# Folding phi's weights in two halves of TensorE's rows, two heads in each

## The chip, the cores and the metric

The kernel runs on one core of one Trainium2 chip. The metric is the device time of one execution in microseconds (us). Before the change three runs took 357.98 us in the median (357.31 to 358.96). The profiled execution is one more, with a time of its own.

## The reference, cut to what matters

Two branches, A and B, each compute linear attention with a learned feature map over the same x (2048 tokens, 448 features, 16 heads of 28), and a gate mixes them:

```python
qkv = (x @ wqkv)                                  # per branch; q, k, v of 16 heads x 28
pq = einsum("bhsd,hdf->bhsf", q, w_phi)           # per head 28 x 28
pk = einsum("bhsd,hdf->bhsf", k, w_phi)
phi_q = concat([softmax(pq), softmax(-pq)])       # and phi_k of pk
kv = einsum("bhsf,bhsd->bhfd", phi_k, v); z = phi_k.sum over s
o = einsum(phi_q, kv) / (einsum(phi_q, z) + 1e-6)
out = g * (oA @ woA) + (1 - g) * (oB @ woB),  g = sigmoid((x * gate_w).sum(-1))
```

w_phi acts on q and k head by head, so x @ wq followed by w_phi is one product with a folded weight: for each head, wq's 28 columns times w_phi's 28 x 28. The kernel computes these folded weights once, for k and for q of each branch (four folds), and then projects x with them.

## The kernel before, in words

**Order of the work.** One program, each engine runs its instructions in the order in which the kernel issues them (`tc.manual_schedule()`). The first loop runs over eight units of 256 tokens for branch A's k and v (state kv), a second loop over eight units does A's q, B's k and v and A's numerators, and a list of steps written by hand does B's queries and the output. Projections (`proj`, L181) are 22 matmuls of 448 or 450 columns per unit in fp32r. `kv_acc` (L245) makes 32 matmuls of 56 columns, whose results go to four strips of 32 PSUM partitions. `num` (L327) makes 32 matmuls of a 32 x 32 weight with 256 columns, in four strips of rows by four strips of columns.

**A fold.** `fold` (L159) takes a weight that lies transposed in SBUF: `wt`, 112 partitions (4 heads x 28) by 4 groups by 512 columns (448 input features and 64 repeated). Group g holds heads 4g to 4g+3. `bd` is a block-diagonal 112 x 112 matrix for each branch and group, made of w_phi by four multiplications with a mask (L399). For each pair of input chunks (c, c+1) and each group, `fold_mm` issues one fp32 matmul: weights are 112 rows x 128 columns of `wt`, the moving operand is `bd`, 112 columns, the result 128 x 112 of a PSUM bank, one bank for each chunk. `fold_out` copies the 128 x 896 result to an fp32r tile on ScalarE (L156) and writes the rest to a second one on VectorE (L157). The profile shows each fp32 matmul as two pairs of a weight load and a matmul, so a fold is 16 matmuls in the program and 32 pairs in the trace.

**The four folds and their sources.** Fold 1 (A's k) stands after the first v projection; its weights come by `load_wt` (L114, DMA L117) in two DMAs of 448 KB, behind the first loads of x and wv and ahead of x for tokens 256 to 511 (`load_x(0, 2, 4)`, xrb) on SP's queue. Fold 2 (A's q) stands in unit 1, fold 3 (B's k) in unit 3, fold 4 (B's q) in unit 0 of the second loop; each of their weights is one DMA of 896 KB, issued long before. The last one (into tile `ctr`) is issued in unit 5, between loads of `wos` and the store of a q tile (`qd`, L281).

**Queues.** SP and ScalarE issue the DMAs, each in its own order. The program gives the DMAs of both queues eight semaphores in turn, so a DMA is not issued before the one eight places ahead of it has landed. ScalarE issues the loads of wp (w_phi, L376) and mask (L377) before its first work, the table load and the split of x (L108).

Of the kernel before, what the change touches and what calls it, by code (L numbers as in the profile page):

```python
# [8 lines left out]
F32 = mybir.dt.float32  # L9
F32R = mybir.dt.float32r  # L10
AF = mybir.ActivationFunctionType
OP = mybir.AluOpType
AX = mybir.AxisListType

P = 128
S, D, H, DH = 2048, 448, 16, 28
# [3 lines left out]
HA = 2 * H  # L20
NP = H // 2
PF = 4 * DH
DG = D + 2
HP = 32
WARM = 21
# [24 lines left out]
def hedgehog_mix(ctx: ExitStack, tc: tile.TileContext, xd, wv, wkt, wqt, wphi, wo, cmask, cpmask, out):  # L50


    nc = tc.nc
# [24 lines left out]
    wp_ = ctx.enter_context(tc.tile_pool(name="wts", bufs=1))  # L78

    res = ctx.enter_context(tc.tile_pool(name="res", bufs=1, side="right"))  # L80
    wtb = [res.tile([P, 2048], F32, name=f"wtb{i}") for i in range(2)]
# [4 lines left out]
    start = ExitStack()  # L86
    raw = start.enter_context(tc.tile_pool(name="raw", bufs=1, side="right"))
    ident = raw.tile([P, P], F32, name="ident")
    make_identity(nc, ident)
    mask = raw.tile([PF, 4], F32, name="mask")  # L90
    wp = raw.tile([PF, 2, 4, HP], F32, name="wp")
    bd = wp_.tile([PF, 2, 4, PF], F32, name="bd")
    wk = [wp_.tile([P, 2, 4, D], F32R, name="wka"), wp_.tile([P, 2, 4, D], F32R, name="wkb")]
    wvs = [wp_.tile([P, 2, 4, DG], F32R, name="wva"), wp_.tile([P, 2, 4, D], F32R, name="wvb")]
    wq = [wp_.tile([P, 2, 4, D], F32R, name="wqa"), None]
# [6 lines left out]
    def load_x(g, lo, hi, eng=nc.sync):  # L102
        eng.dma_start(xraw[g][:, :, lo * P:hi * P], xd[:, g * GT + lo * P:g * GT + hi * P].rearrange("(c p) t -> p c t", p=P))

    def split_x(g, lo, hi, *parts):
        r, t, h = [a[:, :, lo * P:hi * P] for a in (xraw[g], xg[g], xg[g].bitcast(F32))]
        if 0 in parts:
            nc.scalar.activation(t[:, 0:4], r, AF.Copy)  # L108
        if 1 in parts:
            nc.gpsimd.tensor_tensor(t[64:P, 3], r[64:P, 3], h[64:P, 3], OP.subtract)  # L110
        if 2 in parts:
            nc.gpsimd.tensor_tensor(t[:, 4:7], r[:, 0:3], h[:, 0:3], OP.subtract)  # L112

    def load_wt(dst, src, n=4):  # L114
        wt = dst[:PF].rearrange("p (g c) -> p g c", g=4)
        for g in range(0, 4, n):
            nc.sync.dma_start(wt[:, g:g + n], src[g * PF:(g + n) * PF].rearrange("(g p) c -> p g c", p=PF))  # L117
        return wt

    def load_wv(b, c, n=2, eng=nc.sync):  # L120
        w = (DG, D)[b]
        if c % 2 == 0:
            t = raw.tile([P, 2, w], F32, name=f"wvr{c}")
            for i in range(2):
                wvr[c + i] = t[:, i]
            if n == 2:
                return eng.dma_start(t, wv[c * P:(c + 2) * P, b * DG:b * DG + w].rearrange("(c p) n -> p c n", p=P))
        eng.dma_start(wvr[c], wv[c * P:(c + 1) * P, b * DG:b * DG + w])

# [14 lines left out]
    def two_tile(i=None):  # L144
        if i is None:
            i = turn[0] = (turn[0] + 1) % 3
        return twos[i].tile([P, 2, 512], F32, name=f"two{i}")

    def fold_mm(b, wt, ps, g, c):
        for i in range(2):  # L150
            nc.tensor.matmul(ps[:, i, g * PF:(g + 1) * PF], wt[:, g, (c + i) * P:(c + i + 1) * P], bd[:, b, g],  # L151
                             start=True, stop=True)

    def fold_out(ps, dst, c):
        dh, dl = dst[:, 0, c:c + 2], dst[:, 1, c:c + 2]
        nc.scalar.activation(dh, ps[:, :, :D], AF.Copy)  # L156
        nc.vector.tensor_tensor(dl, ps[:, :, :D], dh.bitcast(F32), OP.subtract)  # L157

    def fold(b, wt, dst):  # L159
        for c in range(0, 4, 2):  # L160
            ps = two_tile()
            for g in range(4):
                fold_mm(b, wt, ps, g, c)
            fold_out(ps, dst, c)

    TERMS = [(c, 0, c) for c in range(3)] + [(4 + c, 0, c) for c in range(3)] + [(3, 0, 3)] + [(c, 1, c) for c in range(4)]
# [5 lines left out]
    def proj(u, w, ps, order=None):  # L172
        n = w.shape[3]
        for i, j in order or [(i, j) for i in range(2) for j in range(11)]:
            if i is None:
                warm(j)
                continue
            t = 2 * u + i
            x, o = xg[t // 4], (t % 4) * P
            xc, k, wc = TERMS[j]  # L180
            nc.tensor.matmul(ps[:, i, :n], x[:, xc, o:o + P], w[:, k, wc], start=j == 0, stop=j == 10)  # L181
        return ps
# [190 lines left out]
    load_x(0, 0, 1)  # L373
    load_wv(0, 0, 1, nc.scalar)
    load_wv(0, 1, 1)
    nc.scalar.dma_start(wp, wphi)  # L376
    nc.scalar.dma_start(mask, cmask)  # L377
    load_wv(0, 2, 1)
    load_wv(0, 3, 1)
    load_x(0, 1, 2)  # L380
    wt = load_wt(wtb[0], wkt[0], 2)
    load_x(0, 2, 4)
    load_x(1, 0, 4)
    for v in vs:
# [10 lines left out]
        high_wv(0, c)  # L395
        low_wv(0, c, nc.vector)
    split_x(0, 1, 2, 0, 1, 2)
    for q in range(4):
        nc.vector.tensor_scalar(bd[:, :, :, q * DH:(q + 1) * DH], wp[:, :, :, :DH], mask[:, q:q + 1], None, op0=OP.mult)  # L399
    pv = proj(0, wvs[0], two_tile(), TERMS0)  # L400
    split_x(0, 2, 4, 0, 1, 2)
    v_out(0, pv)
    fold(0, wt, wk[0])
    split_x(1, 0, 4, 0, 1, 2)
    v_out(1, proj(1, wvs[0], two_tile()))
# [25 lines left out]
    for u in range(NU):  # L431
# [29 lines left out]
        if u == 0:  # L461
            wtqa = load_wt(wtb[0], wqt[0])
            load_x(2, 0, 4)
            for c in range(0, 4, 2):
                load_wv(1, c)
        if u == 1:
            wtkb = load_wt(wtb[1], wkt[1])
            nc.sync.dma_start(wos.rearrange("g (a f) n -> g a (f n)", f=DH),
                              wo.rearrange("(a g f) n -> g a (f n)", g=4, f=DH))
# [21 lines left out]
        if u == 1:  # L491
            fold(0, wtqa, wq[0])
        if u == 3:
            fold(1, wtkb, wk[1])
# [11 lines left out]
    wq[1] = wp_.tile([P, 2, 4, D], F32R, name="wka")  # L506
    ca = wp_.tile([P, 2, 4, DG], F32, name="wva").rearrange("p x c n -> p (x c n)")
    ctr = [ca[:, :2048], None]
# [23 lines left out]
    for u in range(NU):  # L532
        k = NU + u
        f, m, n = u + 2, u + 1, u - 1
# [257 lines left out]
    for step in STEPS.split():  # L792
        name, _, arg = step.partition(".")
# [44 lines left out]
```

## Time and profile before

| | |
|---|---|
| median of three runs | 357.98 us |
| the profiled execution: time / span of its instructions | 359.09 us / 357.2 us |
| TensorE clock granted, mean | 0.998 |
| busy share PE / weight loads (PEld) / VectorE (DVE) / ScalarE (ACT) / GpSimd (POOL) | 97 / 85 / 76 / 34 / 73% |
| moved by DMA | 45.75 MB, 128 GB/s in the mean |
| matmuls of the four folds (L151) | 128 in the trace, 11.3 + 3.8 us busy |

The span runs from the first to the last instruction; the execution's time is 1.9 us longer. In the rows below, PEld is the weight load of TensorE and PE the matmul; `[0.77 <-POOL xg L112]` means that the engine was idle for 0.77 us and that POOL's instruction of line 112, which wrote xg, ended that. Rows ending in q (SPq, ACTq) are the issue of a DMA. "x32" is the number of merged instructions.

### The profile page before, as it was taken

To read this page: it belongs to the slowest core of one execution; us is meant where nothing else is said; L and a number is where in the kernel's file an instruction comes from. 1 tells how busy PE (TensorE), PEld (TensorE's weight loads), DVE (VectorE), ACT (ScalarE), POOL (GpSimd) and SP (SyncE) were. 2 spreads that over 40 slices of the span, in tenths; PEclk is the share of its full clock that TensorE was granted. 3 is DMA by queue.
4 is the path that set the end of the run, shared out by engine and by line. 5 is a ranking of instruction groups with operands and counts; after the bars stand their busy time and mean duration, and the time that the engine had idled before them with its cause. 6 is when DMAs were issued, how large, how long until landed. Compare 5 with 4: busy or idle time off the path is not lost.

```text
span 357.2 us, 8435 instructions
## 1 busy us (share of the span) xinstructions
PE 346.2 (97%) x3599; PEld 304.6 (85%) x3599; DVE 270.1 (76%) x312; ACT 121.8 (34%) x171; POOL 261.5 (73%) x226
## 2 busy tenths in 40 slices
PE   7999899999999999999999999999999999999995
PEld 6889789988987889798898989888888978888894
DVE  4118765643967749998989898899899999988840
ACT  4433532534054241315133131412224454434331
POOL 2453897497476606988889788886779999999850
PEclk9999999999999999999999999999999999999999
DMA  7795225300753402241313332249662461664111
GB/s 236 221 319 173 114 79 193 135 25 14 210 157 141 129 1 61 75 126 61 103 54 104 106 104 65 94 162 352 160 226 84 140 196 57 180 180 128 53 52 51
DMA packets 33733, 45.75 MB, mean 128 GB/s; under 512 B 11408, under 2 KB 27008, under 8 KB 33408
## 3 DMA queue, kind: packets, MB, share of 16 engines
q1 hardware_dynamic: 28688, 41.20, 36.9%
q10 hardware_dynamic: 5008, 4.02, 3.5%
q8 instruction: 28, 0.46, 0.5%
q14 instruction: 9, 0.07, 0.1%
HBM read 27.29 MB, written 19.53 MB: 131 GB/s over the span
## 4 chain that ended last, share of the span: by engine, by line
PE 65%; DMA 12%; POOL 8%; DVE 8%; issue 3%; ACT 2%; SPq 1%; ACTq 0%; POOLq 0%; DVEq 0%
PE two L181 39%; PE out L773 16%; PE two L327 4%; DMA qd<-uq 4%; POOL e L220 3%; PE kv L245 3%; DMA xrb<-in_xt 2%; POOL xg L112 1%; DMA wtb<-wos 1%; DVE sm L211 1%; DVE wtb L315 1%; ACT e L202 1%; DMA wp<-in_wphi 1%; DMA wod<-wtb 1%; PE two L151 1%
## 5 line engine op out<-in xcount | busy, mean ns | idle before, releaser
L181 PE MATMUL two<-wka,xg 128*128 128x448 f32 x352 | 73.8, 365 | 0.0
L181 PEld LDWEIGHTS two<-wka,xg 128*128 128x128 f32 x352 | 65.2, 188 | 5.6 <-issue 0.8
L220 POOL TENSOR_TENSOR e<-e,rs 128x896 f32<-128x896 f32 x32 | 53.9, 1706 | 19.1 <-DVE rs L212 19.1
L228 ACT ACTIVATE vs<-two 128x896 f32<-128x896 f32 x16 | 14.7, 920 | 97.6 <-PE two L181 97.6
L181 PE MATMUL two<-wva,xg 128*128 128x450 f32 x176 | 39.4, 373 | 1.9 <-ACT wva L131 1.0
L211 DVE TENSOR_REDUCE sm<-e 128x32 f32<-128x896 f32 x32 | 33.1, 1077 | 8.6 <-ACT e L202 8.6
L181 PE MATMUL two<-wqa,xg 128*128 128x448 f32 x176 | 38.0, 371 | 1.0 <-DVE wqa L157 1.0
L315 DVE STREAM_TRANSPOSE wtb<-xrb 128x2048 f32<-128x2048 f32 x16 | 36.6, 2290 | 2.3 <-ACT glog L230 2.3
L181 PEld LDWEIGHTS two<-wva,xg 128*128 128x128 f32 x176 | 32.8, 189 | 6.2 <-POOL xg L112 1.1
L181 PE MATMUL two<-wvb,xg 128*128 128x448 f32 x176 | 37.2, 366 | 0.0
L181 PE MATMUL two<-wkb,xg 128*128 128x448 f32 x176 | 36.5, 362 | 0.0
L181 PEld LDWEIGHTS two<-wqa,xg 128*128 128x128 f32 x176 | 32.4, 188 | 4.8 <-DVE wqa L157 1.4
L198 POOL TENSOR_TENSOR e<-mx,e 128x896 f32<-128x896 f32 x16 | 27.3, 1704 | 12.5 <-DVE mx L197 9.2
L181 PEld LDWEIGHTS two<-wvb,xg 128*128 128x128 f32 x176 | 33.0, 188 | 2.7
L181 PEld LDWEIGHTS two<-wkb,xg 128*128 128x128 f32 x176 | 33.0, 188 | 2.3
L773 PE MATMUL out<-wkb,e 128*128 128x448 f32 x154 | 34.7, 369 | 0.1
L202 ACT ACTIVATE e<-e 128x896 f32<-128x896 f32 x32 | 28.7, 945 | 17.7 <-POOL e L198 17.6
L773 PEld LDWEIGHTS out<-wkb,e 128*128 128x128 f32 x154 | 28.5, 188 | 4.1 <-issue 0.8
L305 POOL TENSOR_TENSOR xrb<-qmn,tq 128x896 f32<-128x896 f32 x16 | 28.1, 1758 | 2.7 <-issue 2.2
L272 DVE TENSOR_REDUCE qmx<-two 128x32 f32<-128x896 f32 x14 | 15.1, 1077 | 16.6 <-PE two L181 16.6
L365 POOL TENSOR_TENSOR wva<-wva,cdd 128x896 f32<-128x896 f32 (+1 forms) x12 | 26.5, 2211 | 0.9
L365 POOL TENSOR_TENSOR ctr<-ctr,cdd 128x896 f32<-128x896 f32 (+1 forms) x12 | 26.5, 2209 | 0.6
(105 smaller groups left out, 583.5 us busy)
## 6 DMA issues: line engine op xcount, KB each, us to landing
tq<-qd SPq DMA_DIRECT2D x16, 448.0 KB, 4.7
qd<-uq ACTq DMA_DIRECT2D x32, 112.0 KB, 2.7
qd<-uq SPq DMA_DIRECT2D x32, 112.0 KB, 2.1
od<-wva SPq DMA_DIRECT2D x8, 448.0 KB, 2.5
wqa<-od SPq DMA_DIRECT2D x8, 448.0 KB, 4.4
out<-bd SPq DMA_DIRECT2D x16, 224.0 KB, 3.6
wod<-wtb SPq DMA_DIRECT2D x14, 224.0 KB, 2.0
xrb<-in_xt SPq DMA_DIRECT2D x2, 1024.0 KB
```

The costliest lines, as they stand in the source:

```text
L181: nc.tensor.matmul(ps[:, i, :n], x[:, xc, o:o + P], w[:, k, wc], start=j == 0, stop=j == 10)
L198: nc.gpsimd.tensor_tensor(e5[:, 1], mx[:, 1, :, :, None].to_broadcast([P, 2, H, DH]), e5[:, 0], OP.subtract)
L202: nc.scalar.activation(es[k][:, s], es[k][:, s], AF.Exp)
L211: nc.vector.tensor_reduce(sm[:, s], e[:, s].rearrange("p (h f) -> p h f", f=DH), AX.X, OP.add)
L220: nc.gpsimd.tensor_tensor(e3, e3, rs[:, s, :, None].to_broadcast([P, HA, DH]), OP.mult)
L228: nc.scalar.activation(v[:, :, :, :, :DH].rearrange("p w j q f -> p w (j q) f"), hb(ps[:, :, :D]), AF.Copy)
L272: nc.vector.tensor_reduce(mx, p4, AX.X, OP.max)
L305: nc.gpsimd.tensor_tensor(eq[:, 1, :, :, :DH], mn.rearrange("p c a -> p a c")[:, :, :, None].to_broadcast([P, 8, 4, DH]), tview(k), OP.sub ...
L315: nc.vector.transpose(wtb[k % 2], eq.rearrange("p s a c f -> p (s a c f)"))
L327: nc.tensor.matmul(banks[r][32 * g:32 * g + 32, 256 * s:256 * s + 256], kvt[b][32 * r:32 * r + 32, s, g], eT[32 * r:32 * r + 32, s, g], st ...
L365: nc.gpsimd.tensor_tensor(c3, c3, dd.to_broadcast([P, 8, hi - lo, DH]), OP.mult)
L773: nc.tensor.matmul(outs[t % 2][:, :D], (hi, lo)[x][:, c], w[:, c], start=x == 0 and n == 0 and c == 0, stop=x == 1 and c == 6)
```

## The change

Each group of four heads is split into two pairs. The first pair of every group lies in partitions 0 to 55, the second in 64 to 119, and `bd` holds 56 x 56 block-diagonal matrices in the same two ranges. A matmul of 112 rows and 112 columns becomes two of 56 rows and 56 columns, one in each half of TensorE's rows (the program marks them as tiles of 64 x 128 at rows 0 and 64); the two halves write different PSUM banks. A fold has 32 matmuls in the program in place of 16, in the order chunk, group, half. `load_wt` issues two DMAs of 56 partitions for each weight, wp and mask come in two DMAs each, the four multiplications for `bd` have 56 partitions, and `fold_out` reorders while it copies. Nothing else changes.

```diff
+PG = 2 * DH
+HALVES = [(i, slice(64 * i, 64 * i + PG)) for i in range(2)]
...
-    bd = wp_.tile([PF, 2, 4, PF], F32, name="bd")
+    bd = wp_.tile([P, 2, 4, PF], F32, name="bd")[:, :, :, :PG]
...
+    def load_wt(dst, src):
+        wt = dst.rearrange("p (g c) -> p g c", g=4)
+        for i, rows in HALVES:
+            nc.sync.dma_start(wt[rows], src.rearrange("(g s p) c -> s p g c", s=2, p=PG)[i])
         return wt
...
-    def fold_mm(b, wt, ps, g, c):
-        for i in range(2):
-            nc.tensor.matmul(ps[:, i, g * PF:(g + 1) * PF], wt[:, g, (c + i) * P:(c + i + 1) * P], bd[:, b, g],
-                             start=True, stop=True)
+    def fold_mm(b, wt, ps, c):
+        for j in range(2):
+            for g in range(4):
+                for i, rows in HALVES:
+                    nc.tensor.matmul(ps[:, i, (4 * j + g) * PG:(4 * j + g + 1) * PG], wt[rows, g, (c + j) * P:(c + j + 1) * P],
+                                     bd[rows, b, g], start=True, stop=True)

     def fold_out(ps, dst, c):
-        dh, dl = dst[:, 0, c:c + 2], dst[:, 1, c:c + 2]
-        nc.scalar.activation(dh, ps[:, :, :D], AF.Copy)
-        nc.vector.tensor_tensor(dl, ps[:, :, :D], dh.bitcast(F32), OP.subtract)
+        hi, lo = [dst[:, k, c:c + 2].rearrange("p c (g i f) -> p i (c g) f", g=4, i=2) for k in range(2)]
+        src = ps[:, :, :D].rearrange("p i (a f) -> p i a f", f=PG)
+        nc.scalar.activation(hi, src, AF.Copy)
+        nc.vector.tensor_tensor(lo, src, hi.bitcast(F32), OP.subtract)
...
-    nc.scalar.dma_start(wp, wphi)
-    nc.scalar.dma_start(mask, cmask)
+    for i, rows in HALVES:
+        nc.scalar.dma_start(wp[rows], wphi[i * PG:i * PG + PG])
+        nc.scalar.dma_start(mask[rows], cmask[i * PG:i * PG + PG, 2 * i:2 * i + 2])
...
-    wt = load_wt(wtb[0], wkt[0], 2)
+    wt = load_wt(wtb[0], wkt[0])
```

TensorE's order around fold 4, before (L245 is `kv_acc`, L151 the fold, with the two chunks' PSUM tiles `two`; L181 a projection, L327 `num`):

```order
L181 MATMUL two_1194<-wkb,xg_69 128x448 x22
L245 MATMUL kv<-e,vs_148 29x56 x32
L151 MATMUL two_1260<-bd,ctr 128x112 x8
L151 MATMUL two_1271<-bd,ctr 128x112 x8
L181 MATMUL two_1282<-wvb,xg_69 128x448 x22
```

and with the change:

```order
L186 MATMUL two_1247<-wkb,xg_69 128x448 x22
L250 MATMUL kv<-e,vs_148 29x56 x32
L156 MATMUL two_1313<-bd,ctr 128x56 x16
L156 MATMUL two_1332<-bd,ctr 128x56 x16
L186 MATMUL two_1351<-wvb,xg_69 128x448 x22
```

The place is the same, the matmuls are twice as many with half the columns; line numbers move by five to seven. SP's queue at the start, before (xrb and wtb are x's buffers, wvr the raw wv, L117 the folds' weights):

```order
L128 DMA wvr_157<-in_wv 128x450 x2
L103 DMA xrb<-in_xt 128x4x128
L117 DMA wtb_121<-in_wkt 112x2x512 [waits DMAHW0_49]
L117 DMA wtb_121<-in_wkt 112x2x512 [waits DMAHW1_49]
L103 DMA xrb<-in_xt 128x4x256 [waits DMAHW2_49]
```

and with the change:

```order
L131 DMA wvr_159<-in_wv 128x450 x2
L106 DMA xrb<-in_xt 128x4x128 [waits DMAHW1_49]
L120 DMA wtb_121<-in_wkt 56x4x512 [waits DMAHW2_49]
L120 DMA wtb_121<-in_wkt 56x4x512 [waits DMAHW3_49]
L106 DMA xrb<-in_xt 128x4x256 [waits DMAHW4_49]
```

The two loads of the fold's weights now have 56 partitions and all four groups each, and the semaphores that the DMAs wait for move on by two, because ScalarE issues two DMAs more. ScalarE's start with the change (before, rows 3 and 4 of these DMAs were not there, and none waited):

```order
L131 DMA wvr_152<-in_wv 128x450
L382 DMA wp<-in_wphi 56x256
L383 DMA mask<-in_cmask 56x2
L382 DMA wp<-in_wphi 56x256
L383 DMA mask<-in_cmask 56x2 [waits DMAHW0_49]
L111 ACT_TABLE_LOAD
L111 ACTIVATE xg_69<-xrb 128x4x128 [waits DMAHW1_49]
```

The fourth small load waits for the semaphore of ScalarE's own first DMA (wvr), and the table load stands behind it.

More of the change, by code (lines that the diff above doesn't have):

```diff
@@ L89, in hedgehog_mix @@
     make_identity(nc, ident)
-    mask = raw.tile([PF, 4], F32, name="mask")
-    wp = raw.tile([PF, 2, 4, HP], F32, name="wp")
-    bd = wp_.tile([PF, 2, 4, PF], F32, name="bd")
+    mask = raw.tile([P, 2], F32, name="mask")
+    wp = raw.tile([P, 2, 4, HP], F32, name="wp")
+    bd = wp_.tile([P, 2, 4, PF], F32, name="bd")[:, :, :, :PG]
     wk = [wp_.tile([P, 2, 4, D], F32R, name="wka"), wp_.tile([P, 2, 4, D], F32R, name="wkb")]
@@ L112, in split_x @@
             nc.gpsimd.tensor_tensor(t[:, 4:7], r[:, 0:3], h[:, 0:3], OP.subtract)
[L114 to L117, printed above, removed]
+    def load_wt(dst, src):
+        wt = dst.rearrange("p (g c) -> p g c", g=4)
+        for i, rows in HALVES:
+            nc.sync.dma_start(wt[rows], src.rearrange("(g s p) c -> s p g c", s=2, p=PG)[i])
         return wt
@@ L161, in fold @@
             ps = two_tile()
-            for g in range(4):
-                fold_mm(b, wt, ps, g, c)
+            fold_mm(b, wt, ps, c)
             fold_out(ps, dst, c)
@@ L397, in hedgehog_mix @@
     split_x(0, 1, 2, 0, 1, 2)
-    for q in range(4):
-        nc.vector.tensor_scalar(bd[:, :, :, q * DH:(q + 1) * DH], wp[:, :, :, :DH], mask[:, q:q + 1], None, op0=OP.mult)
+    for q in range(2):
+        for i, rows in HALVES:
+            nc.vector.tensor_scalar(bd[rows, :, :, q * DH:(q + 1) * DH], wp[rows, :, :, :DH], mask[rows, q:q + 1], None, op0=OP.mult)
     pv = proj(0, wvs[0], two_tile(), TERMS0)
```

## The prediction

> **What bounds the kernel now.** I read the page's first part, then the chain that ended last, then the groups of line 151, then the timeline around each of the four folds.
>
> ```profile
> span 357.2 us, 8435 instructions
> PE 346.2 (97%) x3599; PEld 304.6 (85%) x3599; DVE 270.1 (76%) x312; ACT 121.8 (34%) x171; POOL 261.5 (73%) x226
> PE 65%; DMA 12%; POOL 8%; DVE 8%; issue 3%; ACT 2%; SPq 1%; ACTq 0%; POOLq 0%; DVEq 0%
> ```
>
> TensorE is all but always busy, and two thirds of the chain are its own. So a shorter fold could pay, but only where TensorE's work ends last behind it. The next rows are the four folds and what ends the waits behind them.
>
> ```profile
> 13.07 3.72 PE L151 MATMUL two<-bd,wtb 112*128 112x112 f32 x32
> 18.20 4.18 PE L181 MATMUL two<-wva,xg 128*128 128x450 f32 x19 [0.77 <-POOL xg L112]
> 31.03 3.72 PE L151 MATMUL two<-bd,wtb 112*128 112x112 f32 x32
> 40.16 4.75 PE L181 MATMUL two<-wqa,xg 128*128 128x448 f32 x22 [0.98 <-DVE wqa L157]
> 61.44 3.83 PE L151 MATMUL two<-bd,wtb 112*128 112x112 f32 x32
> 65.30 0.92 ACT L156 ACTIVATE wkb<-two 128x896 fp32r<-128x896 f32 x1 [0.29 <-PE two L151]
> 70.06 3.36 POOL L220 TENSOR_TENSOR e<-e,rs 128x896 f32<-128x896 f32 x2 [3.99 <-DVE rs L212]
> 121.26 3.83 PE L151 MATMUL two<-bd,ctr 112*128 112x112 f32 x32
> 139.47 0.27 POOL L359 TENSOR_TENSOR cden<-cden,gate 128x32 f32<-128x32 f32 x1 [1.01 <-DMA gate<-gd]
> ```
>
> Behind fold 1 TensorE waits for x anyway, behind fold 2 for ScalarE's and VectorE's copies. Behind fold 3 only 0.29 us of waiting is the fold's. Fold 4 stands on the chain: what follows it leads by the gate to POOL, which had 1.01 us to wait there.
>
> **Why a fold takes 3.72 us.** These rows give the durations of one load and one matmul (min/median/max in ns) for the fold, for kv and for num.
>
> ```profile
> L151 PEld LDWEIGHTS two<-bd,wtb x96: 186/192/192, 12.9 to 64.9; 112*128 112x128 f32 x96
> L151 PE MATMUL two<-bd,wtb x96: 261/275/363, 13.1 to 65.0; 112*128 112x112 f32 x96
> L245 PEld LDWEIGHTS kv<-e,vs x64: 103/108/108, 44.8 to 45.6; 128*29 128x29 f32 x64
> L245 PE MATMUL kv<-e,vs x64: 212/213/236, 44.9 to 45.6; 128*29 128x56 f32 x64
> L327 PE MATMUL two<-wtb,kvt x64: 374/375/398, 161.3 to 162.4; 32*32 32x256 f32 x64
> 161.31 0.23 PEld L327 LDWEIGHTS two<-wtb,kvt 32*32 32x32 f32 x32 [0.29 <-issue]
> 44.85 0.84 PEld L245 LDWEIGHTS kv<-e,vs 128*29 128x29 f32 x64 [0.32 <-issue]
> 44.85 0.99 PE L245 MATMUL kv<-e,vs 128*29 128x56 f32 x64
> ```
>
> 32 pairs in 3.72 us, less the last one's 275 ns, are 111 ns from start to start. A load costs (192 - 108) / (128 - 29) = 0.85 ns a column, 109 ns for 128 columns. A matmul costs (375 - 213) / (256 - 56) = 0.81 ns a column, 91 ns for 112. The load fits 111 ns, the matmul doesn't. So the fold is bound by loading its weights, and halving the matmul's columns halves what was already hidden.
>
> **The change part by part.**
>
> *The folds' pairs.* There are now 64 pairs a fold, each with a load of 128 columns and a matmul of 56. If the two halves of the rows load at the same time, each half has 32 loads at 111 ns, 3.6 us as before: 0. If they load one after the other, it is 64 x 111 = 7.1 us, +3.4 a fold. If I am wrong about the load and the matmul sets the pace, kv's is the nearest row: (0.99 - 0.213) / 63 = 12.3 ns a pair over four strips, 49 ns in a strip, so 32 x 49 = 1.6 us and -1.9 with the switch below. Between them I take 0, by num's row: 32 loads of 32 columns (27 ns each, 0.86 us one by one) lay within 0.23 us of which a single load takes 0.10, six at a time, more than its four strips of columns, so strips of rows load together.
>
> The Trainium skill, "TensorE: Matmul & The Clock Gate", section "LDWEIGHTS (loading the stationary operand)", says that a load's time goes by its columns and not by its rows, at columns / 1.2 ns; the trace agrees, with 0.85 ns a column. The section speaks against this change: 64 loads of 128 columns would be an estimated 6.8 us a fold one by one, against 3.4 for 32.
>
> *Switching the tiles' shape.* Where TensorE goes from a full array to strips, loads pause: 0.32 us before kv's. Before, a fold's loads follow a projection's without such a pause. I take 0.15 us for each new switch (0 to 0.32). Folds 3 and 4 stand behind kv, which has the switch already, so each gets one at its end: 2 x 0.15 = 0.3 us exposed. Folds 1 and 2 get two each, under the waits of 0.77 and 0.98 us behind them: 0.
>
> *Fold 1's weights.* The start hangs on x for tokens 256 to 511, which queues behind these weights:
>
> ```profile
> 5.57 8.74 DMA xrb<-in_xt
> 14.33 1.07 ACT xg L108
> 16.32 1.83 POOL xg L112
> 18.20 13.02 PE two L181 x63
> wtb<-in_wkt SPq DMA_DIRECT2D x2, 448.0 KB
> 7.50:10.50 3.00, 2.25 (x13) 1.63 (x12) 2.27 (x7) 1.21 (x2) 0.46 (x1) 1.00 1.06 248
> 13.00:14.50 1.50, 1.50 (x15) 1.48 (x14) 0.00 (x0) 0.17 (x1) 0.00 (x0) 1.00 1.05 385
> ```
>
> The last two rows are stretches (their last columns are clock, DMA share and GB/s). While mostly these weights move, all DMA engines are busy at 248 GB/s; while x moves into 128 partitions, at 385. So 112 partitions are filled more slowly than 128. The 896 KB take 3.7 us now. With 56 partitions at a time I take half of 385, 192 GB/s: 4.8 us, +1.1. From below, the full 385 gives 2.4 us, -1.3. From above, the rate could go down with the partitions to 124 GB/s: 7.4 us, +3.7. All of it moves xrb's landing and so the matmuls at 18.20: +1.1.
>
> The Trainium skill, "DMA: Bandwidth & Descriptors", sections "Why a DMA increments its semaphore by 16 and not by 1" and "Rules for kernel authors", says that a DMA runs on as many engines, up to 16, as divide the slowest dimension, 14 for 56, and that two transfers to disjoint halves of the partitions are not worth making. By that alone, 248 x 14/16 = 217 GB/s is an estimated 4.2 us and +0.5. No run here shows the engines yet.
>
> *ScalarE's start.*
>
> ```profile
> 1.76 0.45 ACTq L377 DMA_DIRECT2D mask<-in_cmask  x1
> 2.24 1.28 ACT L108 ACT_TABLE_LOAD   x1 [2.24 <-issue]
> 4.51 0.63 ACT L108 ACTIVATE xg<-xrb 128x512 fp32r<-128x512 f32 x1 [0.98 <-DMA xrb<-in_xt]
> 4.22 0.83 SPq L117 DMA_DIRECT2D wtb<-in_wkt  x2
> ```
>
> The fourth small load now waits for the first wvr load. SP's L117, issued at 4.22, waited for the same semaphore, so it lands at about 4.2. Then come 0.45 us of issue and 1.28 of table: ScalarE starts at about 6.0 in place of 4.51, and everything queued behind it on ScalarE (wva's splits, on which TensorE's first matmuls wait) starts 1.5 us later. That lies before the wait that ends at 18.20; the 0.77 us there and the 1.1 that x is late cover it: 0, and up to 0.7 if x is not late.
>
> *The other three weights.* SP issues one DMA more each. For folds 2 and 3 the weights land long before they are used: 0. Fold 4's stand ahead of a store of q:
>
> ```profile
> 92.10 0.47 SPq L117 DMA_DIRECT2D ctr<-in_wqt  x1
> 93.66 10.12 DMA qd<-uq
> 103.90 0.34 SPq L289 DMA_DIRECT2D tq<-qd  x1
> 105.77 4.21 DMA wod<-wtb
> 110.11 2.31 DVE wtb L315
> 120.34 0.99 PE kv L245 x64
> ```
>
> The q load at 103.90 waits until that store has landed, SP's stores of wod stand behind it, and the transpose at 110.11 waits for the last of them. One more issue (0.33 to 0.47 us) or a longer transfer moves this: +0.35 (0 to 1.1, if the transfer loses as much as fold 1's).
>
> *bd and the copies.* The four multiplications keep their 224 elements a partition: 0. `fold_out` copies as many elements as before; a copy that reorders in the same way, v's, has the same time:
>
> ```profile
> L156 ACT ACTIVATE wka<-two 128x896 fp32r<-128x896 f32 x4 | 3.6, 921 | 2.5 <-PE two L151 2.5
> L228 ACT ACTIVATE vs<-two 128x896 f32<-128x896 f32 x16 | 14.7, 920 | 97.6 <-PE two L181 97.6
> ```
>
> Sum: 0 + 0.3 + 1.1 + 0.35 = +1.75 us on the span of 357.2, 358.95. The profiled execution took 359.09 us, 1.9 more than its span and 1.1 more than the median; against the median the sum gives 357.98 + 1.75 = 359.7. Of this kernel a measurement can tell about 0.5% (1.8 us) from no change.
>
> **The rivals.**
>
> *The matmuls set the pace* (chance 0.11). Folds of 1.8 us give nothing behind folds 1 and 2, at most the 0.29 us behind fold 3, and 1.0 (POOL's wait for the gate) to 1.9 at fold 4: -1.3 to -2.2. With the loads' cost that is about 358.0, without it 356.2. For it speaks that kv's strips keep 49 ns; against it the 111 ns that fit the load alone. It decides as soon as a fold is under 3.4 us.
>
> *The halves load one after the other* (0.13): the change doesn't do what it says. Each fold then takes 7.2 us, +3.4. Fold 1 ends at 20.3 and holds the work at 18.20 by 1.6 beyond the late x; fold 2 loses 3.4 - 0.98 = 2.4; folds 3 and 4 lose all: 1.6 + 2.4 + 3.4 + 3.4 = 10.8, with the 1.75 about 370.5, slower. Num's row speaks against it, but its strips are 32 columns wide. It decides above 4.0 us a fold.
>
> *The loads are no slower* (0.12). Two transfers fill both halves in turn as fast as now, and only the switches remain: 357.98 + 0.3 = 358.3. Against it speaks that 112 partitions are already slower than 128.
>
> **How the numbers follow.** The forecast (folds as long as now, loads slower) has 0.62, with its bounds from 357.98 - 1.3 = 356.7 to 357.98 + 0.3 + 3.7 + 0.35 = 362.3; 0.02 is left for what I don't see. The range 356.8 to 362.5 holds it, the rival with unchanged loads and most of the faster one; it leaves out the serial loads and some of the rest, 2 in 10. The forecast lies at the edge of 0.5%: half of its chance is slower (0.31), half the same (0.31). Serial loads add 0.13 to slower, unchanged loads 0.11 to same, the faster rival 0.08 to faster and 0.03 to same; with the rest split that makes faster 0.10, same 0.45, slower 0.45.
>
> **What would show it.** Right: a fold of 128 matmuls' loads, 64 pairs in 3.6 to 4.0 us, a load's duration near 190 ns, a pause of loads behind each fold, xrb's landing at about 15.4, the wait before the matmuls now at 18.20 ending at about 19.3, ScalarE's first copy at about 6. Wrong: 64 pairs in under 3.4 us (the load is cheaper with half the rows) or over 4.5 (the halves take turns); xrb landing at 14.3 or earlier.

## The result and the profile after

The changed kernel takes 361.14 us (median of 8 runs, 359.61 to 362.94), the kernel before 357.60 (8 runs): a ratio of 1.0104, 95% interval 1.0080 to 1.0128. It is slower by more than the 0.5% that can be told from no change. The prediction had 359.7, with 356.8 to 362.5.

The 8 runs are of two kinds. Four have a mean granted clock of 0.999 or 1.000: 359.61, 359.65, 360.14 and 360.47 us. The other four have 0.986 to 0.994: 361.82 to 362.94 us. The profile is of the run of 360.47 us, so it shows only the first kind. Ratios below leave out the executions that are slow beside the others of their kernel (one of 56 of the kernel before, 424.82 us at a clock of 0.755; one of six with the small load later, 369.84; two of four with half the columns on full rows, 387.22 and 387.35), so there a ratio is not that of the medians. The page begins with the span and the busy times, and the chain's shares by engine.

```profile
span 358.7 us, 8697 instructions
PE 348.1 (97%) x3727; PEld 306.5 (85%) x3727; DVE 271.7 (76%) x312; ACT 121.6 (34%) x171; POOL 262.2 (73%) x226
PE 70%; DVE 7%; POOL 7%; DMA 7%; issue 3%; ACT 3%; SPq 2%; ACTq 0%; DVEq 0%; POOLq 0%
```

TensorE's share of the chain is 70% (65% before). The next rows are the durations of a fold's loads and matmuls (min/median/max in ns), and then TensorE's timeline at the four folds and behind them.

```profile
L156 PEld LDWEIGHTS two<-bd,wtb x192: 182/188/188, 14.4 to 65.4; 56*128 56x128 f32 x192
L156 PE MATMUL two<-bd,wtb x192: 272/272/313, 14.4 to 65.5; 56*128 56x56 f32 x192
```

```profile
14.42 3.78 PE L156 MATMUL two<-bd,wtb 56*128 56x56 f32 x64
18.13 4.79 PE L186 MATMUL two<-wva,xg 128*128 128x450 f32 x22
31.67 3.78 PE L156 MATMUL two<-bd,wtb 56*128 56x56 f32 x64
40.71 4.54 PE L186 MATMUL two<-wqa,xg 128*128 128x448 f32 x21 [0.64 <-DVE wqa L163]
61.98 3.78 PE L156 MATMUL two<-bd,wtb 56*128 56x56 f32 x64
121.37 0.99 PE L250 MATMUL kv<-e,vs 128*29 128x56 f32 x64 [0.92 <-POOL e L225]
122.29 3.78 PE L156 MATMUL two<-bd,ctr 56*128 56x56 f32 x64
126.00 4.75 PE L186 MATMUL two<-wvb,xg 128*128 128x448 f32 x22
```

64 pairs take 3.78 us, as 32 did (3.72 to 3.83). Behind fold 1 the matmuls at 18.13 run on without the wait for x: here TensorE itself is late. Its start is seen in these rows of the timeline (ACT's queue, ACT, PE twice, then x's landing at ACT).

```profile
4.34 0.32 ACTq L383 DMA_DIRECT2D mask<-in_cmask  x1
4.70 1.28 ACT L111 ACT_TABLE_LOAD   x1 [4.70 <-DMA wvr<-in_wv]
5.99 0.63 ACT L111 ACTIVATE xg<-xrb 128x512 fp32r<-128x512 f32 x1
7.14 0.74 PE L186 MATMUL two<-wva,xg 128*128 128x450 f32 x1 [1.06 <-ACT wva L134]
7.68 0.63 PE L396 MATMUL two<-ident 128*128 128x128 f32 x2
14.59 1.06 ACT L111 ACTIVATE xg<-xrb 128x1024 fp32r<-128x1024 f32 x1 [5.58 <-DMA xrb<-in_xt]
```

ScalarE starts at 5.99 in place of 4.51, TensorE waits 1.06 us for wva, and fold 1 begins 1.35 us later. But that wait alone doesn't make fold 1 late. The kernel before with only its small loads split (second run below) waits nearly as long, and its fold 1 begins at 12.98, no later than the 13.07 of the trace of before:

```profile
7.06 0.48 PE L181 MATMUL two<-wva,xg 128*128 128x450 f32 x1 [0.97 <-ACT wva L131]
7.37 0.38 PE L391 MATMUL two<-ident 128*128 128x128 f32 x2
12.98 3.72 PE L151 MATMUL two<-bd,wtb 112*128 112x112 f32 x32
```

The difference is in the first matmuls: 0.74 and 0.63 us in the changed kernel's trace, 0.48 and 0.38 there. The traces' records of the clock begin with a step to full clock, at 10.29 us in this trace, 6.08 with the small loads split and 4.37 before; ahead of that step the profile's clock column reads 1.00, but the matmuls are slow. So in this execution most of fold 1's delay is TensorE's late step to full clock. The last place is the q store, in the chain of waits.

```profile
92.64 0.50 SPq L120
93.18 0.85 SPq L120
94.56 10.98 DMA qd<-uq
105.62 0.34 SPq L294
```

The q load goes out at 105.62 in place of 103.90, and kv's matmuls at 121.37 in place of 120.34.

### The profile page after: what moved, and what is told of

Same layout as the page of the kernel before. It is cut to its first block, busy times and chain, and to the rows that moved or that the text cites. A ratio compares the mean times of both kernels' runs of the same rounds, so it can differ in the third digit from the quotient of the medians.

```text
span 358.7 us, 8697 instructions
## 1 busy us (share of the span) xinstructions
PE 348.1 (97%) x3727; PEld 306.5 (85%) x3727; DVE 271.7 (76%) x312; ACT 121.6 (34%) x171; POOL 262.2 (73%) x226
## 4 chain that ended last, share of the span: by engine, by line
PE 70%; DVE 7%; POOL 7%; DMA 7%; issue 3%; ACT 3%; SPq 2%; ACTq 0%; DVEq 0%; POOLq 0%
PE two L186 42%; PE out L780 16%; PE two L332 4%; PE kv L250 3%; PE two L156 3%; DMA qd<-uq 3%; POOL e L225 3%; POOL e L203 1%; DMA wod<-wtb 1%; DVE wtb L320 1%; DVE sm L216 1%; DMA wvr<-in_wv 1%; ACT e L207 1%; POOL xg L115 1%; DMA gd<-glog 1%
## 5 line engine op out<-in xcount | busy, mean ns | idle before, releaser
L225 POOL TENSOR_TENSOR e<-e,rs 128x896 f32<-128x896 f32 x32 | 53.9, 1704 | 19.3 <-DVE rs L217 19.3
```

The lines of the kernel that those rows point to most:

```text
L225: nc.gpsimd.tensor_tensor(e3, e3, rs[:, s, :, None].to_broadcast([P, HA, DH]), OP.mult)
```

## The experiments

Each group below shares its runs of the kernel before: medians of 357.50, 357.49 and 357.46 us, and a mean clock of 0.997 or more in 55 of 56. Times are medians, ratios stand with their 95% intervals.

### First theory: ScalarE's late start

The first theory (S below) was that ScalarE's late start costs both the time on the chain and the clock. The rivals were the weights' loads (W) and the folds' matmuls (F).

**One small load later.**

```diff
     for i, rows in HALVES:
         nc.scalar.dma_start(wp[rows], wphi[i * PG:i * PG + PG])
-        nc.scalar.dma_start(mask[rows], cmask[i * PG:i * PG + PG, 2 * i:2 * i + 2])
+        if i == 0:
+            nc.scalar.dma_start(mask[rows], cmask[i * PG:i * PG + PG, 2 * i:2 * i + 2])
...
         low_wv(0, c, nc.vector)
+    nc.scalar.dma_start(mask[HALVES[1][1]], cmask[PG:2 * PG, 2:4])
```

> The changed kernel, with one of its four small loads (the second half of mask) issued by ScalarE behind wva's splits, so that it holds up nothing. Theories: (S) the loss comes from ScalarE's late start, which TensorE meets in its first matmuls; (W) it comes from fold 1's weights, which are loaded in two halves of 56 partitions; (F) it comes from the folds' matmuls in halves of the rows, which draw down TensorE's clock. S expects ScalarE's first copy at about 4.5 us, the first matmul at about 5.7, the second half of the x19 matmuls behind fold 1 at about 18.4 with a wait for x in front of it again (about +0.25 against the kernel before, what is left of the weights' load), a span of about 358.0 to 358.4, a median of 358.3 to 359.7 and a granted clock of 0.998 or more in every execution. W expects the chain behind fold 1 still 0.5 us later than before, and with F a median near 361 with executions of a clock below 0.995.

367.30 us, ratio 1.0248 (1.0209 to 1.0286), with clocks of 0.969 to 0.991. No theory's expectation held. The rows of ScalarE's queue, of VectorE and of TensorE say why.

```profile
6.88 0.32 ACTq L404 DMA_DIRECT2D mask<-in_cmask  x1
14.32 1.05 DVE L408 TENSOR_SCALAR bd<-wp,mask 56x224 f32<-56x224 f32 x3 [5.21 <-DMA mask<-in_cmask]
15.06 7.44 PE L156 MATMUL two<-bd,wtb 56*128 56x56 f32 x64 [2.89 <-DVE bd L408]
```

```profile
16.00:16.50 0.50, 0.50 (x8) 0.50 (x7) 0.00 (x0) 0.03 (x1) 0.42 (x2) 0.50 0.05 16
```

ScalarE did start early, but the moved 0.4 KB, issued at 6.88 behind the weights and x, landed only at 14.3, and TensorE idled for 2.89 us. Then fold 1 took 7.44 us, twice its time, at a granted clock of 0.50 (the number before the last two in the row of a half microsecond). So this run doesn't price ScalarE's start; it shows the halved clock in a fold.

**The small loads alone**, split in the kernel before:

```diff
-    nc.scalar.dma_start(wp, wphi)
-    nc.scalar.dma_start(mask, cmask)
+    for i in (0, 56):
+        nc.scalar.dma_start(wp[i:i + 56], wphi[i:i + 56])
+        nc.scalar.dma_start(mask[i:i + 56], cmask[i:i + 56])
```

> The kernel before, with wp and mask loaded in two halves of 56 partitions each (four small loads on ScalarE's queue in place of two); folds and weights as before. S (ScalarE's late start) expects its first copy at about 6.0 us, TensorE's first matmul at about 7.1, +0.5 on the chain behind fold 1 (about 18.7 in place of 18.20), and a median slower by 0.5 (time on the chain alone) to 3.5 us (if the idle TensorE also lowers the granted clock in some executions, then to 0.986 to 0.995 as in the changed kernel). W (weights' loads) and F (folds in halves) expect the time of the kernel before, 357.6 within 0.5, and clocks of 0.997 and above.

358.41 us, ratio 1.0022 (1.0009 to 1.0035): the split costs 0.9 us where nothing else is late. That is not ScalarE's start alone: the edit moves the semaphores of SP's queue too, and in its trace SP issues x's second load at 4.64 us in place of 2.70 and fold 1's weights at 5.07 in place of 4.22. Two of 12 clocks are below 0.997 (0.994 and 0.996). The time is at the lower end of S, and the late start is at most a small part of the low clocks.

**The weights' loads alone**, in the kernel before:

```diff
-        for g in range(0, 4, n):
-            nc.sync.dma_start(wt[:, g:g + n], src[g * PF:(g + n) * PF].rearrange("(g p) c -> p g c", p=PF))
+        for i in (0, 56):
+            nc.sync.dma_start(wt[i:i + 56], src.rearrange("(g s p) c -> s p g c", s=2, p=56)[i // 56])
```

> The kernel before, with each of the four weights wtb loaded in two DMAs of 56 partitions (rows 0 to 55 and 56 to 111) with all four groups; fold 1's weights were two DMAs of 112 partitions, the others one. Folds as before. W (the weights' loads) expects xrb's landing 0.3 us or more later, the matmuls behind fold 1 later by the same, +0.46 at the state's matmuls by the late q store, so +0.7 us at the end of the span, and, if these loads are the whole of the loss, +1.5 on the span and +2 to +3.5 on the median. S (ScalarE's late start) expects x later by the same 0.3 us and +0.5 in the middle: a median of 358.0 to 358.6, with clocks as in the kernel before. F (folds in halves) expects the same as S.

359.73 us, ratio 1.0062 (1.0039 to 1.0085), all clocks 0.998 or more. The loads cost 2.2 us, more than S expected and less than the whole. Its chain of waits has x's transfer and the matmuls behind it, and its timeline fold 1 waiting for its own weights.

```profile
5.37 9.97 DMA xrb<-in_xt
19.25 13.02 PE two L181 x63
```

```profile
14.29 3.80 PE L151 MATMUL two<-bd,wtb 112*128 112x112 f32 x32 [1.06 <-DMA wtb<-in_wkt]
```

x lands at 15.34, and the matmuls come at 19.25, 1.05 later than in the trace of the kernel before.

**A longer warm-up** in the changed kernel (`WARM = 30` in place of 21).

> The changed kernel with 30 transposes in the warm-up in place of 21, so that TensorE doesn't idle from 6.1 to 7.1 us while it waits for wva. S expects the first matmul still at 7.1 to 7.8 us (the time on the chain stays: span 358.5 to 359.3), and, if the idle 1 us in the warm-up is what lowers the granted clock in some executions, clocks of 0.998 or more in all of them and a median of 359.5 to 360.2. If the clock has another cause (F, the folds' halves), the median stays near 361 with executions at 0.986 to 0.995.

361.32 us, ratio 1.0102 (1.0064 to 1.0140), clocks of 0.980 to 0.992 in six of seven executions. TensorE was busy until the first matmul of a projection, and the clock fell all the same: S is out as the cause of the clock. This trace caught a stretch at half the clock. First fold 2 on TensorE's timeline, then half microseconds behind its middle (columns: the stretch and its length, busy time of PE, PEld, DVE, ACT, POOL, the clock, DMA share, GB/s).

```profile
31.38 4.11 PE L156 MATMUL two<-bd,wtb 56*128 56x56 f32 x64
```

```profile
34.00:34.50 0.50, 0.50 (x14) 0.50 (x13) 0.50 (x1) 0.50 (x3) 0.00 (x0) 1.00 0.00 0
34.50:35.00 0.50, 0.50 (x10) 0.50 (x10) 0.50 (x2) 0.50 (x2) 0.10 (x1) 0.68 0.00 0
35.00:35.50 0.50, 0.50 (x7) 0.40 (x5) 0.50 (x1) 0.43 (x1) 0.50 (x1) 0.50 0.93 401
...
37.50:38.00 0.50, 0.50 (x3) 0.46 (x2) 0.00 (x0) 0.50 (x2) 0.46 (x1) 0.50 0.00 0
38.00:38.50 0.50, 0.50 (x4) 0.47 (x3) 0.00 (x0) 0.50 (x2) 0.50 (x1) 0.91 0.00 0
```

A mean of 0.68 is full clock for 0.18 of the 0.50 us, one of 0.91 half clock for 0.09: the clock is 0.50 from 34.68 to 38.09, 3.4 us, though TensorE is busy all the time. It begins within fold 2.

### Second theory: the folds themselves

From here on the theory (H) is that a fold in halves lets the clock be halved for 3.4 us in some executions. Two runs split the change in two: the folds' matmuls alone, and all the rest.

**The folds alone**, in the kernel before. This kernel leaves rows 56 to 63 of each group out of the folds, so its second half has 48 rows:

```diff
+                for i, rows in enumerate((slice(0, 56), slice(64, 112))):
+                    nc.tensor.matmul(ps[:, i, (4 * j + g) * 56:(4 * j + g + 1) * 56], wt[rows, g, (c + j) * P:(c + j + 1) * P],
+                                     bd[rows, b, g, 56 * i:56 * i + 56], start=True, stop=True)
```

> The kernel before with its loads of weights, wp and mask as they were, and only the folds' matmuls changed: 64 pairs a fold, in the halves of TensorE's rows, 56 columns each, on rows 0 to 55 and 64 to 111 of the weights (so rows 56 to 63 of each group, and the heads' parts in them, are left out of the folds). Theory H: the folds in halves let the chip halve TensorE's clock for stretches of 3.4 us in some executions, as in the run with the longer warm-up (from 34.7 to 38.1 us, at the end of fold 2). H expects clocks of 0.98 to 0.995 in a third or more of the executions, and a median of 358.0 to 360.0. Theory L: the whole loss comes from the loads and ScalarE's start; L expects 357.5 within 0.5 and clocks of 0.997 and above. The time on the chain from the folds alone at full clock is expected at 0 to +0.3.

359.46 us, ratio 1.0061 (1.0036 to 1.0085), seven of nine clocks at 0.995 or less. H holds, L falls. The nine times go by the clock: 357.90 and 358.06 at 1.000; 359.09, 359.26 and 359.46 at 0.995; 359.75 at 0.994; 359.86 at 0.992; 360.83 at 0.989; 362.38 at 0.983. One stretch of 3.4 us at half the clock takes 1.7 / 357 = 0.005 off the mean clock, and by these times costs about 1.3 us. It doesn't always: with the longer warm-up the two executions at 0.992, the profiled one among them, took 359.48 and 359.56 us, the one at 0.999 359.72. (In that trace the half clock from 355.5 us to the end of the span takes another 0.003 off the mean.) The profiled execution of the folds alone (0.995) has one such stretch. Its fold 1 on TensorE's timeline, and the 1 us stretches behind it:

```profile
12.22 3.78 PE L153 MATMUL two<-bd,wtb 56*128 56x56 f32 x64
```

```profile
16.00:17.00 1.00, 1.00 (x5) 0.79 (x5) 0.63 (x2) 0.95 (x2) 0.58 (x1) 0.70 0.00 0
17.00:18.00 1.00, 1.00 (x5) 0.87 (x4) 1.00 (x1) 1.00 (x1) 0.00 (x0) 0.50 0.90 119
18.00:19.00 1.00, 1.00 (x4) 0.91 (x3) 0.09 (x1) 0.77 (x1) 0.10 (x1) 0.50 0.97 358
19.00:20.00 1.00, 1.00 (x4) 0.88 (x4) 0.00 (x0) 0.00 (x0) 1.00 (x1) 0.59 1.05 289
20.00:21.00 1.00, 1.00 (x7) 0.92 (x6) 0.00 (x0) 0.00 (x0) 0.92 (x2) 1.00 1.08 299
```

It runs from 16.4 to 19.8: the projection behind the fold pays, with 4 or 5 matmuls a microsecond in place of 7.

**All but the folds**: the edits of the small loads alone and of the weights' loads alone, together.

> The kernel before with all of the change except the folds' matmuls: weights in two loads of 56 partitions, wp and mask in two halves on ScalarE's queue. H (clock through the folds in halves): clocks of 0.997 and above in all executions, and a median of 359.5 to 360.2, that of the changed kernel's executions at full clock (359.6 to 360.5). If ScalarE's late start or the loads lower the clock: executions at 0.986 to 0.995 and a median near 361.

359.69 us, ratio 1.0062 (1.0049 to 1.0074), all clocks 0.997 or more, as H expects. It is no slower than the weights' loads alone (359.73): where the weights are late, ScalarE's late start costs nothing more.

**The halves one after the other**, in the changed kernel:

```diff
-        for j in range(2):
-            for g in range(4):
-                for i, rows in HALVES:
+        for i, rows in HALVES:
+            for j in range(2):
+                for g in range(4):
```

> The changed kernel with the folds' loops in another order: for each pair of chunks all 8 matmuls of the first half of the rows, then all 8 of the second half, in place of the halves in turn. If two halves load at the same time only because they alternate, the loads of one half now follow each other: 64 loads of 111 ns, 7.1 us a fold in place of 3.65 (behind fold 1 some of it under the wait for x), and a median of 368 to 372. If each half's loads were in truth half as long (a price by rows), or TensorE fetches the other half's loads far ahead, the fold stays at 3.7 to 4.5 us and the median at 360 to 363.

**Half the columns on full rows**, in the kernel before:

```diff
-            nc.tensor.matmul(ps[:, i, g * PF:(g + 1) * PF], wt[:, g, (c + i) * P:(c + i + 1) * P], bd[:, b, g],
-                             start=True, stop=True)
+            for h in (0, 56):
+                nc.tensor.matmul(ps[:, i, g * PF + h:g * PF + h + 56], wt[:, g, (c + i) * P:(c + i + 1) * P], bd[:, b, g, h:h + 56],
+                                 start=True, stop=True)
```

> The kernel before, with each fold matmul of 112 columns cut into two of 56 columns on the same 112 rows and the same weights (64 pairs a fold, each with its own load). If a fold is bound by its loads: 64 x 111 ns = 7.1 us a fold; fold 1 then ends at about 20.2 in place of 18.20 (+2.0), fold 2 loses 3.4 - 0.98 = 2.4, folds 3 and 4 lose 3.4 each: +11, a median of 368 to 370. If it is bound by its matmuls (56 columns at 0.81 ns and less than 49 ns of fixed cost): 3.1 to 3.9 us a fold and a median of 357 to 358.5. If what halves TensorE's clock in the changed kernel is little matmul work a fold's time (and not the halves of the rows), the clock goes down here too, to 0.99 or less; if it is the halves of the rows, it stays at 0.997 or more.

382.99 us, ratio 1.0714 (1.0674 to 1.0754), and 386.41 us, ratio 1.0719 (1.0662 to 1.0776). Their fold 1, from each TensorE's timeline and the microsecond in which the clock goes down:

```profile
12.94 6.68 PE L156 MATMUL two<-bd,wtb 56*128 56x56 f32 x64
```

```profile
18.00:19.00 1.00, 1.00 (x9) 1.00 (x8) 0.39 (x1) 0.00 (x0) 0.07 (x1) 0.69 0.06 8
```

```profile
12.17 9.82 PE L152 MATMUL two<-bd,wtb 112*128 112x56 f32 x64
```

```profile
16.00:17.00 1.00, 1.00 (x9) 1.00 (x8) 0.17 (x1) 0.80 (x1) 1.00 (x1) 0.73 0.00 0
```

In the first the clock is full until 18.38, so the 6.68 us are 5.44 + 1.24 / 2 = 6.1 at full clock; its pairs start 112 ns apart within a half, and three pairs overlap at each change of halves. In the second the clock is half from 16.46 on: 4.29 + 5.53 / 2 = 7.1 us at full clock, 110 ns a pair. So a fold is bound by its loads of 128 columns, and two halves load at the same time only when they are issued in turn. Both medians lie 11 us or more above the 368 to 372 us that were expected of this alone, and the clocks (0.950 to 0.966) say why: they fall with full rows too. So little matmul work for a load brings the half clock, and the halves of the rows are not needed for it.

**The zero columns back**, in the changed kernel:

```diff
-    bd = wp_.tile([P, 2, 4, PF], F32, name="bd")[:, :, :, :PG]
+    bd = wp_.tile([P, 2, 4, PF], F32, name="bd")
...
-                    nc.tensor.matmul(ps[:, i, (4 * j + g) * PG:(4 * j + g + 1) * PG], wt[rows, g, (c + j) * P:(c + j + 1) * P],
+                    nc.tensor.matmul(ps[:, i, (4 * j + g) * PG:(4 * j + g + 2) * PG], wt[rows, g, (c + j) * P:(c + j + 1) * P],
...
+    nc.vector.memset(bd[:, :, :, PG:], 0.0)
```

> The changed kernel, with each fold matmul's columns back at 112: 56 of the block and 56 of zeros, which the next matmul overwrites; still two matmuls in the halves of TensorE's rows. Theory C (the half-clock stretches come from too little matmul work in a fold: 56 columns to a load of 112 ns) expects clocks of 0.997 and above in all executions and the time of the run with all but the folds, 359.7 within 0.6. Theory R (they come from working in halves of the rows) expects clocks of 0.98 to 0.995 in a third or more of the executions and about 361, as in the changed kernel. Both expect a fold of 3.7 to 3.9 us if the halves' matmuls run side by side; if they run in turn, a fold takes 64 x 91 ns = 5.8 us and the median goes to 364 to 367.

359.42 us, ratio 1.0068 (1.0043 to 1.0094): the time of all but the folds, as C expects. C also expected a clock of 0.997 or more in every execution; it is so in five of seven (four of eight of the changed kernel, two of nine with the folds alone). In the profiled one of the other two, the slowest of the seven with 363.0 us, TensorE idled 1.53 us behind fold 1's first two pairs:

```profile
15.02 5.42 PE L156 MATMUL two<-bd,wtb 56*128 56x112 f32 x62 [1.53 <-DMA wtb<-in_wkt]
64.21 3.83 PE L156 MATMUL two<-bd,wtb 56*128 56x112 f32 x64
```

There the half clock follows the idle time: the stretches of 1 us have it from 15.9 to 19.4. Fold 3's 3.83 us show that the halves' matmuls also run side by side: in turn they would take 5.8. Whether the halves have a part of their own in the second low clock stays open; it has no trace. The padded halves below have the zero columns too, and their four clocks are 0.997 or more: nine of eleven in all, against seven of 24 in the changed kernel, with the longer warm-up and with the folds alone.

The traces also show where a stretch can begin. Counted from the step to full clock at the start, the half clock sets in after 27.31 us (8 x 3.413) with the longer warm-up and after 10.24 (3 x 3.413) with the folds alone. Of the 3.41 us just ahead, 3.30 and 3.01 lie in a fold. With all but the folds, such a stretch of time (61.94 to 65.35 us) lies wholly in fold 3, and one (125.17 to 128.58) wholly in fold 4 with the zero columns, and the clock stays full behind both. So where the folds lie on this grid of 3.41 us may decide which executions lose clock. It isn't the whole rule, since 3.14 us of fold 4 in the changed kernel's trace were not followed by a loss, and no run tests it.

### The weights' rate and fold 4's weights

**Padded weights** in the kernel before: fold 1's weights into all 128 partitions.

```diff
-    wt = load_wt(wtb[0], wkt[0], 2)
+    wt = wtb[0].rearrange("p (g c) -> p g c", g=4)
+    for g in range(0, 4, 2):
+        nc.sync.dma_start(wt[:, g:g + 2], bass.AP(wkt.tensor, g * PF * 512, [[512, P], [PF * 512, 2], [1, 512]]))
+    wt = wt[:PF]
```

> The kernel before, with fold 1's weights loaded into all 128 partitions (the 16 rows above 112 are filled with the first rows of the next group, which no matmul reads): two DMAs of 512 KB in place of two of 448 KB. If a load into 112 partitions is slower because of their number (248 GB/s, against 365 to 389 for x into 128), 1 MB at 375 GB/s takes 2.8 us in place of 3.7: xrb lands 0.9 us earlier, at 13.2 to 13.6 by the kernel before's trace, the matmuls behind fold 1 start 0.8 us earlier and the median is 356.4 to 357.0. If the rate belongs to the weights' place or layout in HBM, 1 MB takes 4.2 us: xrb lands 0.5 later and the median is 357.7 to 358.2.

**Padded halves**: the zero columns back, and fold 1's weights in two loads of 64 partitions.

```diff
-    wt = load_wt(wtb[0], wkt[0])
+    wt = wtb[0].rearrange("p (g c) -> p g c", g=4)
+    for i in range(2):
+        nc.sync.dma_start(wt[64 * i:64 * i + 64], bass.AP(wkt.tensor, i * PG * 512, [[512, 64], [PF * 512, 4], [1, 512]]))
```

> The changed kernel with the zero columns back (as in the run before it), and fold 1's weights loaded as two DMAs of 64 partitions in place of 56 (8 rows of padding in each). If the low rate of the halves (193 to 241 GB/s) comes from 56 partitions, which is no multiple of 16, 64 partitions bring the rate to that of 128, 365 GB/s or more: 1 MB in 2.8 us in place of 4.4, xrb lands at 13.2 to 13.8 and the median is 358.0 to 359.0. If it comes from loading half of the partitions at a time, xrb lands at 14.6 to 15.5 and the median stays at 359.5 to 360.5.

**Padded weights, and fold 4's weights later**: the first of these edits, and in the loop over u

```diff
-            wtqb = load_wt(mid.tile([P, 2048], F32, name="ctr"), wqt[1])
+            ctr0 = mid.tile([P, 2048], F32, name="ctr")
...
         if u == 7:
+            wtqb = load_wt(ctr0, wqt[1])
             q_turn(0)
```

> The kernel before, with fold 1's weights padded to 128 partitions, and fold 4's weights loaded later (behind the q store, the q load and the stores of wod on SP's queue, as the last step of the seventh turn). If both terms hold, padding gives 0.8 us at the start, and the one issue less (0.47 us) ahead of the q store gives 0.3 to 0.5 us at the state's matmuls: a median of 356.0 to 356.7, faster than both kernels. If another wait takes over in the middle, the same as with padding alone. If fold 4's weights now come too late (they have some 12 us before fold 4), slower than that.

They take 357.25 us, ratio 0.9991 (0.9980 to 1.0002); 360.73 us, ratio 1.0092 (1.0079 to 1.0105); and 357.11 us, ratio 0.9989 (0.9981 to 0.9998). The same stretch of the start (GB/s last) in the trace of the folds alone (112 partitions), then of the padded weights (128), with a row of TensorE's timeline behind it, and of the padded halves (64 at a time), with a row of ScalarE's:

```profile
7.00:9.00 2.00, 2.00 (x12) 1.62 (x12) 2.00 (x5) 1.19 (x2) 0.44 (x2) 1.00 1.07 290
```

```profile
7.00:9.00 2.00, 2.00 (x14) 1.64 (x13) 2.00 (x5) 1.22 (x2) 0.35 (x2) 1.00 1.05 384
```

```profile
15.75 4.77 PE L181 MATMUL two<-wva,xg 128*128 128x450 f32 x22
```

```profile
7.00:9.00 2.00, 1.86 (x11) 1.59 (x12) 1.88 (x2) 2.00 (x5) 1.53 (x2) 1.00 0.91 228
```

```profile
15.03 1.06 ACT L111 ACTIVATE xg<-xrb 128x1024 fp32r<-128x1024 f32 x1 [6.02 <-DMA xrb<-in_xt]
```

128 partitions fill at 384 GB/s, 112 at 290, 64 at a time at 228. The padded weights save 0.2 us, not 0.8, and the interval holds no change: TensorE never stops in front of the matmuls at 15.75, and in the folds-alone trace, with the old loads, it didn't either (at 15.93). Padding the halves doesn't help; x lands at 15.03. The later weights of fold 4 take the q store off the chain, but POOL's e and DVE take its place: kv's matmuls come at 118.16, against 118.25 with padding alone. The last version is faster than the changed kernel; its 0.1% against the kernel before are less than the 0.5% that can be told from no change.

## Why the prediction was right, and where not

The direction and the range were right; that the loss would be clear of 0.5% had a chance of 0.45, no more than that it would not. The likeliest time, 359.7, is that of the executions at full clock (median 359.9); the measured median is 1.4 above it, and that part was not in the sum. That the time at full clock came out is in part luck: the sum starts from 357.98, 0.4 above the median of eight runs, and its largest term was too small.

*The folds' pairs, 0: right.* 3.78 us, loads of 188 ns. The halves load together because the code alternates them; one after the other, and on full rows, a pair costs 110 to 112 ns. Both rivals by the fold's time fall, and so does the one with loads no slower (+2.2 us with the loads alone). "Halving the matmul's columns halves what was already hidden" holds for the time, and missed what the hidden columns do: they kept the clock up.

*The clock: missing.* The prediction's list of costs has no step for it. Of the 3.5 us, 2.2 are the loads (all but the folds, 359.69 against 357.49), 0.2 is what the changed kernel's executions at full clock lie above that, and the rest, some 1.1, is half-clock stretches behind folds whose matmuls have 56 columns to a load of 112 ns. The trace of before could not show it: its folds keep the clock.

The Trainium skill, "TensorE: Matmul & The Clock Gate", section "What's actually happening", says that the clock is either full or half, decided in free-running windows of 3.41 us by how busy TensorE was. The stretches here agree: 0.50, for 3.4 us, in some executions and not in others. Its section "HAM oscillation — how this bites in real kernels" asks for no idle gap of more than about 3.4 us; here the clock fell with TensorE busy throughout (0.50 of each 0.50 us in the rows above), so by that rule alone no loss would have come.

*Switching the tiles' shape, +0.3: right in size.* From kv's start to the projection behind fold 4 it is 126.00 - 121.37 = 4.63 us, and 4.51 before: 0.12 for a switch, against 0.15. The folds alone at full clock (two executions) give 357.98 against 357.49, +0.5.

*Fold 1's weights, +1.1: mechanism and rate right, size too small.* The rate was put at 192 GB/s; it is 207 to 213 between 7 and 13 us. With the loads alone x lands at 15.34 (15.4 was forecast) and the matmuls come at 19.25 (19.3). In the changed kernel's own trace neither sign came: x lands at 14.59, and the matmuls run on at 18.13 without a wait. The failed step is "Behind fold 1 TensorE waits for x anyway". That is so in the trace of before, which the prediction itself put 1.1 us above the median. With the same loads in the folds-alone run:

```profile
12.77 1.06 ACT L108 ACTIVATE xg<-xrb 128x1024 fp32r<-128x1024 f32 x1 [4.12 <-DMA xrb<-in_xt]
15.93 6.33 PE L182 MATMUL two<-wva,xg 128*128 128x450 f32 x22
```

x lands 1.56 us earlier there and TensorE has no wait. Against that start the changed kernel's matmuls, at 18.13, are 2.2 us late, the size of the measured loss at full clock. In that trace the slow first matmuls set this as much as x does; with the longer warm-up, whose fold 1 begins at 13.29, TensorE waits 0.57 us for x again, until 18.45. That the usual execution of before starts like this one is inferred from its median and from the padded weights' small gain; it was not traced again.

The Trainium skill's rule of 14 engines for 56 partitions ("DMA: Bandwidth & Descriptors", section "Why a DMA increments its semaphore by 16 and not by 1") gave 217 GB/s, near the measured rate, but is not what is slow: 64 partitions, which 16 divides, fill at 228 GB/s, about as slowly. What its section "Rules for kernel authors" says, that two loads into disjoint halves are not worth making, agrees.

*ScalarE's start, 0: right with the late weights, and only there.* First copy at 5.99 (6.0 was forecast). The split alone costs 0.9 us, SP's later issues included, for which the prediction had no term; "up to 0.7 if x is not late" is near it. Together with the weights' loads it costs nothing more. In the changed kernel's own trace the cover is the other way round: x lands at 14.59 and TensorE is the later one, by its late step to full clock.

*The other weights, +0.35: right.* kv's matmuls come 1.03 us later, 0.56 of it from upstream (84.86 against 84.30 at the kv before): +0.47. How much of the q load's +1.72 reaches TensorE depends on POOL and DVE, which stand close behind.

*bd and the copies, 0: right.* The reordering copy takes as long as the plain one.

```profile
L162 ACT ACTIVATE wka<-two 128x896 fp32r<-128x896 f32 x4 | 3.7, 919 | 3.3 <-PE two L156 3.3
```

## What to carry to other kernels

Look for which of load and matmul sets the pace before cutting columns: here the columns saved were hidden already, and 56 zero columns cost 0.05 us a fold (3.83 against 3.78) and kept the clock full in more of the executions. Before trusting a wait in a profile, hold its execution's own time against the median; a cover that is there in one trace can be gone in the usual run. A load that fills all 128 partitions can be faster than one that leaves 16 out, even with more bytes.

## What the runs showed that I had not expected

- TensorE's clock halves for 3.4 us with TensorE busy throughout, behind folds of 56-column matmuls: seven of nine executions with the folds alone, none of 55 of the kernel before, none of six with all but the folds. The traced stretches begin whole multiples of 3.41 us behind the first step to full clock.
- That first step comes at 4.37 us in the trace of before and at 10.29 in that of the changed kernel, and the matmuls ahead of it are slow though the profile's clock column reads 1.00.
- 896 KB into 112 partitions move at 243 to 290 GB/s, 1 MB into 128 at 366 to 386.
- A load of 0.4 KB issued behind over 2 MB of others landed 7.4 us after its issue.
- With the same loads at the start, x lands at 12.77 us in one trace and at 14.33 in another.
